# First layer in chunk groups of 2, 4, 4, 4, 2, with TensorE's order in the first group written out and the norm's scaling read from PSUM

## Chip, cores and metric

One core of a Trainium2 chip (trn2). The metric is the device time of one execution in microseconds, as the median of several runs; the time of the kernel before is 1269.53 us, the median of three runs from 1269.15 to 1269.59 us.

## The reference

```python
kv  = einsum('bhsd,bhse->bhde', k, v)            # B=4, H=8, S=576, D=64
out = einsum('bhsd,bhde->bhse', q, kv)
x   = out / sqrt(mean(out*out, -1) + 1e-6) * g   # -> [2304 tokens, 512]
h = x @ w_in                                     # 512 -> 2048, float64 weights
x = where(h > 0, h, exp(min(h, 0)) - 1) @ w_out  # 2048 -> 512
p = probs / (probs.sum(-1) + 1e-9)               # 4 experts
y = sum over e of p[:, e] * (relu(x @ w1[e]) @ w2[e])   # 512 -> 1024 -> 512
```

Three stages in a row: attention without softmax and with a norm per head, layer 1 with ELU, layer 2 with four weighted experts.

## The kernel before

The 2304 tokens are 18 tiles of 128, and these are 6 blocks (j) of T = 384 tokens. Every product is made of three matmuls on operands split into a high and a low part: hi·hi, hi·lo, lo·hi (`split`: the high part is a cast on ACT, the low part a subtraction on POOL or DVE). The program is written engine by engine through a framework that schedules the instructions itself: the order in which the functions are called is a priority, and a scheduler with a model of times decides what each engine issues next. After that every engine works through its own queue in order; loads and stores all go through SP's queue.

**Attention.** `emit_kv` multiplies the k and v tiles into ps_kv, the products of a batch are copied to kvd. `emit_o` multiplies a q tile with kvd into ps_o (L316), squares it (ACT, L324), copies it to x (ACT, L325), sums the squares (DVE, L326), forms mean + 1e-6 (L327, on POOL for ten tiles, on DVE for eight), takes the power −0.5 (POOL, L330) and scales x with it (L331, on POOL for nine tiles, on DVE for nine). `emit_x` transposes x on TensorE into ps_xT (L343) and splits the result, times g, into the high (ACT, L352) and low parts (DVE, L353) of xq, the operand of layer 1, 128x256 at a time.

**Layer 1.** d_ff is 16 chunks of 128. They are taken in 4 groups of 4; in a group each block j in turn gets its chunks: `emit_mm1` (12 matmuls into ps_h, L376 to L378), ELU (ACT, ACT, DVE L384), split into h, and two steps later `emit_mm2` (12 matmuls into the four banks ps_y, L395 to L397). After a block's last chunk of a group the four banks are copied to (first group, ACT L405) or added into (DVE, L407) the block's sum acc. A weight chunk arrives as 512 KB of float64 bits in one of two raw buffers, is turned into float32 by five DVE and two ACT steps (`float32_of`, L159 to L175) and split (`split_w`). Attention's steps hang on the steps of the first group by a table, `todo`: tile 17's xT comes with step 13 of 24.

**Layer 2** works on pairs of blocks. `make_forms` makes seven sums and differences ("forms") of a pair's quarter blocks of acc, splits them and stores them to DRAM; `stage_w1` (L203 to L206, DVE) and `split_w1` do the same for the weights. `emit_q` multiplies forms into ps_a, ps_b, ps_c (L422 to L424), `emit_m` makes the second product, weighted into acc (DVE, L488) with the probabilities that `emit_p` loads and normalizes. The forms of the first pair and the probabilities are called in layer 1's last group, 2 to 20 half steps into it.

Of the kernel before, what the change touches and what calls it, by code (L numbers as in the profile page):

```python
# [30 lines left out]
def attention_moe_kernel(  # L31
# [49 lines left out]
    form_p = ctx.enter_context(tc.tile_pool(name="form", bufs=8))  # L81
    raw_p = ctx.enter_context(tc.tile_pool(name="raw", bufs=2))
    w_p = ctx.enter_context(tc.tile_pool(name="w", bufs=NSLOT))
    tf_p = ctx.enter_context(tc.tile_pool(name="tf", bufs=1))
# [4 lines left out]
    x_p = layer1.enter_context(tc.tile_pool(name="x_late", bufs=4, side="right"))  # L89
    cv_p = layer1.enter_context(tc.tile_pool(name="cv", bufs=2, side="right"))  # L90
    h1_p = layer1.enter_context(tc.tile_pool(name="h1", bufs=3, side="right"))
# [15 lines left out]
    g_sb = const.tile([P, 1], F32, name="g_sb")  # L107
    ebias = const.tile([P, 2], F32, name="ebias")
# [4 lines left out]
    p_sb = const.tile([P, NTILE, E], F32, name="p_sb")  # L113
# [13 lines left out]
    groups = []  # L127
    w_in, w_out = w_in.bitcast(U32), w_out.bitcast(U32)
    for g in range(F1 // FG):
        groups.append((w_in, w_out, g * NF))  # L130
    N1 = len(groups)
    for g in range(E * F2 // FG):
        groups.append((w1, w2, g * NF))
    NG = len(groups)
# [3 lines left out]
    def load_w(g, ab, c):  # L138

        if (g, ab, c) in raws or g >= NG:  # L140
            return
        wide = 2 if g < N1 else 1
        r = raws[g, ab, c] = raw_p.tile([P, 512 * wide], U32 if g < N1 else F32, tag="raw", name="raw")
        n = groups[g][2] + c
        nc.sync.dma_start(out=r, in_=groups[g][ab][n * P:(n + 1) * P, :])

    def weights(g, ab, c):
        load_w(g, ab, c)
        r = raws[g, ab, c]
        return float32_of(r) if g < N1 else r  # L150

# [32 lines left out]
    def split_w(g, ab, c):  # L184

        r = weights(g, ab, c)
        w = wf[g, ab, c] = w_p.tile([P, 2, 512], F32R, tag="w", name="w")
        split(w[:, 0, :], w[:, 1, :], r, nc.gpsimd)
# [4 lines left out]
    staged = {}  # L193

    def stage_w1(g, f):

        if g >= NG:
            return
        r0, r1 = weights(g, 0, 2 * f), weights(g, 0, 2 * f + 1)
        tf = tf_p.tile([P, 4, HK], F32, tag="tf", name="tf")  # L200
        b11, b21, b12, b22 = r0[:, :HK], r0[:, HK:], r1[:, :HK], r1[:, HK:]
        sub = nc.vector.tensor_tensor
        sub(out=tf[:, 0, :], in0=b12, in1=b11, op=ALU.subtract)  # L203
        sub(out=tf[:, 2, :], in0=b22, in1=b12, op=ALU.subtract)
        sub(out=tf[:, 1, :], in0=b22, in1=tf[:, 0, :], op=ALU.subtract)
        sub(out=tf[:, 3, :], in0=b21, in1=tf[:, 1, :], op=ALU.subtract)  # L206
        staged[g, f] = r0, r1, tf

    def split_w1(g, f):
# [3 lines left out]
        w = wf[g, 0, f] = [w_p.tile([P, 2, 2, HK], F32R, tag="w", name="w1f") for _ in range(4)]  # L213
# [4 lines left out]
        split(w[3][:, 0, 0], w[3][:, 1, 0], r1[:, HK:], nc.gpsimd)  # L218

# [7 lines left out]
    def make_forms(p):  # L227
# [4 lines left out]
        def form(name, src, eng):  # L232
            if name not in fs:
                fs[name] = form_p.tile([P, 2, 2, T], F32R, tag="f", name="f")
# [5 lines left out]
        def sums(in0, in1, op, into=None):  # L240
            if into is None:
                if "h" in late:
# [18 lines left out]
    def load_forms(p):  # L261
        fs = forms[p] = {}
        for name in F_ORDER:
            f = fs[name] = form_p.tile([P, 2, 2, T], F32R, tag="f", name="f")
# [16 lines left out]
    def emit_kv(t, tags="cd"):  # L281
# [4 lines left out]
        for b, rows in parts(t):  # L286
            first, last = t == tiles_of[b][0], t == tiles_of[b][-1]
            if first:
                kv_bank[b] = bank(tags, "ps_kv")
# [13 lines left out]
        if t + 6 < NTILE:  # L303
            load("k", t + 6)
            load("v", t + 6)

    xn = {}

    def emit_o(t, tags="cd"):

        ps = bank(tags, "ps_o")
        load("q", t)
        qt = main["q", t].rearrange("p (n t) -> p n t", t=P)
        for hp in range(NHP):
# [5 lines left out]
        x = xn[t] = at_p.tile([P, H, D], F32, tag="x", name="x", bufs=5)  # L320
        sq = at_p.tile([P, H, D], F32, tag="sq", name="sq")
        s = at_p.tile([P, H], F32, tag="ss", name="ss", bufs=3)
        ps3 = ps.rearrange("p (h d) -> p h d", d=D)
        nc.scalar.activation(sq, ps3, AF.Square)  # L324
# [5 lines left out]
        nc.gpsimd.tensor_tensor(out=s, in0=s, in1=mhalf, op=ALU.pow)  # L330
# [3 lines left out]
        if t + 6 < NTILE:  # L334
            load("q", t + 6)

    def emit_x(t, tags="cd"):

        x = xn.pop(t)
# [21 lines left out]
    def new_acc(j, shape):  # L361
        acc[j] = (acc_p if j < 2 else late["acc"]).tile(shape, F32, tag=f"acc{j}", name="acc")
# [5 lines left out]
    def emit_mm1(g, j, c):  # L368
        ps = bank("ab", "ps_h")[:, :T]
        w = wf[g, 0, c]  # L370
        for kk in range(KD):
            cols = slice(kk * P, (kk + 1) * P)
            ah, al = w[:, 0, cols], w[:, 1, cols]
            x = xq[j][kk // 2]
            bh, bl = x[:, 0, kk % 2, :], x[:, 1, kk % 2, :]
# [3 lines left out]
        h = hs[g, j, c] = h1_p.tile([P, 2, T], F32R, tag="h", name="h")  # L379
# [6 lines left out]

    def emit_mm2(g, j, c):
        h, w = hs.pop((g, j, c)), wf[g, 1, c]
        hi, lo, bh, bl = h[:, 0, :], h[:, 1, :], w[:, 0, :], w[:, 1, :]
        first, last = c == 0, c == NF - 1  # L390
        if first:
            banks2[j] = [bank("efghcd" if "acc" in late else "efgh", "ps_y")[:, :T] for _ in range(KD)]
        for m, ps in enumerate(banks2[j]):
            cols = slice(m * P, (m + 1) * P)
            nc.tensor.matmul(ps, bh[:, cols], hi, start=first, stop=False)  # L395
            nc.tensor.matmul(ps, bh[:, cols], lo, start=False, stop=False)  # L396
            nc.tensor.matmul(ps, bl[:, cols], hi, start=False, stop=last)  # L397
# [67 lines left out]
    def emit_m(g, p, i):  # L465
# [3 lines left out]
        for c in range(NF):  # L469
            h, w = hs.pop((g, p, c, i)), wf[g, 1, c]  # L470
# [32 lines left out]

# [146 lines left out]
```

## Time and profile before

| | |
|---|---|
| median of three runs | 1269.53 us (1269.15 to 1269.59) |
| the profiled execution, its own time | 1270.84 us |
| its span in the profile | 1269.1 us, 16851 instructions |
| TensorE (PE) busy | 1219.2 us, 96% of the span |
| VectorE (DVE) busy | 616.5 us, 49% |
| ScalarE (ACT) busy | 454.9 us, 36% |
| GpSimd (POOL) busy | 383.7 us, 30% |
| chain that ended last | PE 88%, DVE 3%, POOL 2%, ACT 2%, DMA 2% |

The span is the time from the first to the last instruction that the profiler saw in one execution. A share is an average over stages with different limits: 96% of TensorE says nothing of where the other 4% lie, so the views by stretch of time are read first. A row of the view of groups gives the instruction's line, engine, operation, what it writes and reads, its shape and count, then its busy time in us and the mean of one in ns, and behind the second bar the idle time ahead of it with what ended it. The trace lacks a few per cent of the matmul records, so counts of matmuls are taken from the program.

### The profile page before, as it was taken

Reading aid. Unit: us, or ns where it says so; the run is one execution under the profiler, and the core shown is the slowest. Engines: PE = TensorE matmul, PEld = TensorE weight load, DVE = VectorE, ACT = ScalarE, POOL = GpSimd, SP = SyncE. Lnnn points to the kernel's source line nnn. Section 1 sums busy time; section 2 is a strip of 40 time slices with the busy share of each in tenths; the row PEclk is TensorE's granted clock in tenths of the full one; section 3 lists DMA queues with packets and bytes.
Section 4 is the critical chain, followed back from the end, with each engine's and each line's share of the span. In section 5 each row is a group of like instructions: output and inputs, shape, how many; then the busy total and the mean of one; then the engine's idle time right before and its main releaser. Section 6 shows DMA issues by size and latency. Waiting matters only on the chain.

```text
span 1269.1 us, 16851 instructions
## 1 busy us (share of the span) xinstructions
PE 1219.2 (96%) x6600; PEld 1130.8 (89%) x6600; DVE 616.5 (49%) x1019; ACT 454.9 (36%) x894; POOL 383.7 (30%) x330
## 2 busy tenths in 40 slices
PE   5789779999999999999999999999999999999998
PEld 4678779999999999899899898898898898888887
DVE  4776637427322262566445445445445445444443
ACT  3666546535434354334222222222222222222120
POOL 3465544325323374235203213212212222221000
PEclk9899889999999999999999999999999999999999
DMA  9623103102000041045541441441541441440551
GB/s 324 221 96 108 30 22 86 48 1 65 11 1 9 26 188 37 26 185 206 198 175 50 191 174 51 191 174 50 191 175 50 191 178 47 191 183 17 199 199 75
DMA packets 43887, 147.14 MB, mean 116 GB/s; under 512 B 7072, under 2 KB 7072, under 8 KB 43808
## 3 DMA queue, kind: packets, MB, share of 16 engines
q1 hardware_dynamic: 43808, 146.07, 31.9%
q8 instruction: 52, 0.85, 0.3%
q14 instruction: 27, 0.22, 0.1%
HBM read 124.82 MB, written 21.23 MB: 115 GB/s over the span
## 4 chain that ended last, share of the span: by engine, by line
PE 88%; DVE 3%; POOL 2%; ACT 2%; DMA 2%; issue 1%; SPq 0%; ACTq 0%; DVEq 0%; POOLq 0%
PE ps_y L475 11%; PE ps_y L476 11%; PE ps_y L477 10%; PE ps_y L396 5%; PE ps_y L397 5%; PE ps_y L395 5%; PE ps_h L376 5%; PE ps_h L377 4%; PE ps_h L378 4%; PE ps_a L422 3%; PE ps_a L424 3%; PE ps_a L423 3%; PE ps_c L423 3%; PE ps_c L424 3%; PE ps_c L422 3%; PE ps_b L424 3%
## 5 line engine op out<-in xcount | busy, mean ns | idle before, releaser
L476 PE MATMUL ps_y<-w,h 128*128 128x512 f32 x576 | 226.6, 393 | 0.0
L475 PE MATMUL ps_y<-w,h 128*128 128x512 f32 x576 | 225.4, 394 | 0.6 <-DVE acc L488 0.4
L477 PE MATMUL ps_y<-w,h 128*128 128x512 f32 x576 | 220.4, 395 | 0.0
L449 POOL TENSOR_TENSOR c<-u,p 128x384 f32<-128x384 f32 x48 | 48.8, 1017 | 411.9 <-DVE h L461 411.9
L461 DVE SCALAR_TENSOR_TENSOR h<-c,h 128x384 fp32r<-128x384 f32 x144 | 98.2, 682 | 138.1 <-ACT h L460 138.1
L180 POOL TENSOR_TENSOR h<-e,h 128x384 fp32r<-128x384 f32 x96 | 104.0, 1084 | 186.3 <-ACT h L179 169.0
L460 ACT ACTIVATE h<-c 128x384 fp32r<-128x384 f32 x144 | 75.5, 525 | 203.5 <-DVE c L446 72.6
L376 PE MATMUL ps_h<-x,w 128*128 128x384 f32 x384 | 131.9, 347 | 8.0 <-ACT w L179 4.3
L396 PE MATMUL ps_y<-h,w 128*128 128x384 f32 x384 | 131.0, 341 | 2.3 <-POOL h L180 2.3
L378 PE MATMUL ps_h<-x,w 128*128 128x384 f32 x384 | 131.6, 343 | 1.2 <-POOL w L180 1.2
L377 PE MATMUL ps_h<-x,w 128*128 128x384 f32 x384 | 132.0, 344 | 0.0
L397 PE MATMUL ps_y<-h,w 128*128 128x384 f32 x384 | 128.9, 341 | 0.0
L477 PEld LDWEIGHTS ps_y<-w,h 128*128 128x128 f32 x576 | 108.3, 188 | 22.6
L475 PEld LDWEIGHTS ps_y<-w,h 128*128 128x128 f32 x576 | 108.5, 188 | 20.5 <-DVE acc L488 0.8
L476 PEld LDWEIGHTS ps_y<-w,h 128*128 128x128 f32 x576 | 108.5, 188 | 20.2
L395 PE MATMUL ps_y<-h,w 128*128 128x384 f32 x384 | 124.1, 343 | 1.6 <-ACT acc L405 1.6
L488 DVE SCALAR_TENSOR_TENSOR acc<-ps_y,p_sb,acc 128x512 f32<-128x512 f32 x126 | 88.2, 745 | 72.7 <-PE ps_y L477 72.1
L384 DVE SCALAR_TENSOR_TENSOR e<-e,ps_h 128x384 f32<-128x384 f32 x96 | 52.7, 550 | 143.8 <-ACT e L383 137.2
L376 PEld LDWEIGHTS ps_h<-x,w 128*128 128x128 f32 x384 | 73.9, 193 | 10.3 <-ACT w L179 4.6
L382 ACT ACTIVATE e<-ps_h 128x384 f32<-128x384 f32 x96 | 47.0, 491 | 100.4 <-PE ps_h L378 95.7
L438 ACT COPY p<-ps_c 128x384 f32<-128x384 f32 x48 | 23.0, 480 | 148.2 <-PE ps_c L424 148.2
L378 PEld LDWEIGHTS ps_h<-x,w 128*128 128x128 f32 x384 | 74.1, 193 | 1.7 <-POOL w L180 1.7
(100 smaller groups left out, 2419.3 us busy)
## 6 DMA issues: line engine op xcount, KB each, us to landing
f<-kept SPq DMA_DIRECT2D x98, 768.0 KB, 7.9
raw<-in_moe_w_dram SPq DMA_DIRECT2D x64, 256.0 KB, 2.6
kept<-f SPq DMA_DIRECT2D x21, 768.0 KB, 3.6
raw<-in_moe_w_in_dram SPq DMA_DIRECT2D x16, 512.0 KB, 3.6
raw<-in_moe_w_out_dram SPq DMA_DIRECT2D x16, 512.0 KB, 3.7
qkv<-in_v_dram SPq DMA_DIRECT2D x18, 256.0 KB, 5.3
qkv<-in_k_dram SPq DMA_DIRECT2D x18, 256.0 KB, 5.4
qkv<-in_q_dram SPq DMA_DIRECT2D x18, 256.0 KB, 4.2
```

Of the source, the lines that this page charges most:

```text
L180: eng.tensor_tensor(out=lo, in0=src, in1=hi.bitcast(F32), op=ALU.subtract)
L376: nc.tensor.matmul(ps, ah, bh, start=(kk == 0), stop=False)
L377: nc.tensor.matmul(ps, ah, bl, start=False, stop=False)
L378: nc.tensor.matmul(ps, al, bh, start=False, stop=(kk == KD - 1))
L395: nc.tensor.matmul(ps, bh[:, cols], hi, start=first, stop=False)
L396: nc.tensor.matmul(ps, bh[:, cols], lo, start=False, stop=False)
L397: nc.tensor.matmul(ps, bl[:, cols], hi, start=False, stop=last)
L424: nc.tensor.matmul(ps, wl, xh, start=False, stop=stop and last, skip_group_check=True)
L461: nc.vector.scalar_tensor_tensor(out=lo, in0=ps, scalar=0.0, in1=hi.bitcast(F32), op0=ALU.max, op1=ALU.subtract,)
L475: nc.tensor.matmul(ps, hi[:, cols], bh, start=first, stop=False)
L476: nc.tensor.matmul(ps, hi[:, cols], bl, start=False, stop=False)
L477: nc.tensor.matmul(ps, lo[:, cols], bh, start=False, stop=last)
```

## The change

1. Layer 1's 16 chunks are taken in groups of 2, 4, 4, 4 and 2 in place of 4, 4, 4, 4. There are five groups, so five times instead of four a block's ps_y goes to acc: 24 more adds on DVE.
2. In the first group the matmuls of TensorE are tied together in the order in which they are called, by dependencies that cost no semaphore. The order per block j is: two o tiles of block j+1, `emit_mm1` of the first chunk, the third o tile, half of block j−1's ps_y (`emit_half`, two banks, both chunks), `emit_mm1` of the second chunk, some kv, the three xT of block j+1, the other half of ps_y. The other engines' orders are still the scheduler's.
3. The norm: `emit_o` squares ps_o, sums, adds 64·1e-6 (DVE for all tiles) and takes the power on POOL; `emit_x` scales straight from ps_o in PSUM on DVE (L325). The copy on ACT and the scalings on POOL are gone; the factor 8 that stands for the mean is in g8 = 8·g. The xT is split by one operation of 128x512 each on ACT and DVE (L338, L339).
4. Loads of k, v, q and of the first weights are called by a list. The first w_in chunk stands ahead of k and v tiles 2 to 4 on SP's queue.
5. The form buffers take the space of layer 1's x after layer 1; so `make_forms(0)` and `emit_p` are called behind the loop of layer 1. Layer 1's x, one tile per block, has six buffers, h four instead of three, acc four early ones instead of two.

```diff
-    POOL_MEAN = (1, 2, 3, 5, 8, 9, 12, 14, 16, 17)
-    POOL_SCALE = (2, 6, 8, 9, 10, 13, 15, 16, 17)
...
+    first_groups = [[0, 1]] + [list(range(n, n + NF)) for n in range(2, NC1 - 2, NF)] + [[NC1 - 2, NC1 - 1]]
...
     def emit_o(t, tags="dgh"):
...
         nc.scalar.activation(sq, ps.rearrange("p (h d) -> p h d", d=D), AF.Square)
-        nc.scalar.copy(x, ps3)
         nc.vector.tensor_reduce(out=s, in_=sq, op=ALU.add, axis=AX.X)
-        (nc.gpsimd if t in POOL_MEAN else nc.vector).tensor_scalar(
-            out=s, in0=s, scalar1=1.0 / D, scalar2=1e-6, op0=ALU.mult, op1=ALU.add
-        )
+        nc.vector.tensor_scalar_add(s, s, D * 1e-6)
         nc.gpsimd.tensor_tensor(out=s, in0=s, in1=mhalf, op=ALU.pow)
-        (nc.gpsimd if t in POOL_SCALE else nc.vector).tensor_tensor(
-            out=x, in0=x, in1=s.unsqueeze(2).to_broadcast([P, H, D]), op=ALU.mult
-        )
     def emit_x(t, tags="dgh"):
+        x = at_p.tile([P, H, D], F32, tag="x", name="x")
+        nc.vector.tensor_tensor(
+            out=x, in0=ps_o.pop(t).rearrange("p (h d) -> p h d", d=D),
+            in1=xn.pop(t).unsqueeze(2).to_broadcast([P, H, D]), op=ALU.mult,
+        )
...
-        for kh in range(2):
-            hi, lo = (xq[j][kh][:, a, :, i * P:(i + 1) * P] for a in (0, 1))
-            src = pt3[:, 2 * kh:2 * kh + 2, :]
-            nc.scalar.mul(hi, src, g_sb)
+        hi, lo = (xq[j][:, a, :, i * P:(i + 1) * P] for a in (0, 1))
+        nc.scalar.mul(hi, pt3, g8)
...
+    loads("k0-1 w1c0 k2-4 q0-2 w1c1")
...
+    for j in range(NB):
+        o = list(range(TT * (j + 1), TT * (j + 2))) if j + 1 < NB else []
+        for t in o[:2]:
+            emit_o(t)
+        emit_mm1(j, 0)
+        for t in o[2:]:
+            emit_o(t)
+        if j == 0:
+            split_w(0, 1, 0)
+        if j:
+            emit_half(j - 1, (0, 1))
+        emit_mm1(j, 1)
+        for t in more_kv.get(j, ()):
+            emit_kv(*t)
+        if j == 0:
+            split_w(0, 1, 1)
+        for t in o:
+            emit_x(t)
+        if j == NB - 2:
+            end_attention()
+        if j:
+            emit_half(j - 1, (2, 3))
...
+    emit_half(NB - 1, range(KD))
+    before = None
+    for i in traced[begin:]:
+        if isinstance(i, mybir.InstMatmult):
+            if before is not None:
+                tc.add_manual_dep(
...
     layer1.close()
+    late["form"] = ctx.enter_context(tc.tile_pool(name="form", bufs=8, side="right", reuse_waits="tile"))
...
+    make_forms(0)
+    emit_p()
```

What the two schedules make of it stands in the order of instructions of each engine; three places are shown. The first is TensorE's start, before: kv of the first batch, the first block's o, the first xT, and then the first layer-1 matmuls (ps_h).

```order
L294 MATMUL ps_kv<-qkv 64x64 x48
L316 MATMUL ps_o<-kvd,qkv 128x128 x12
L294 MATMUL ps_kv<-qkv 64x64 x24
L343 MATMUL ps_xT<-ident,x 128x128 x4
L294 MATMUL ps_kv<-qkv 64x64 x8
L343 MATMUL ps_xT<-ident,x 128x128 x8
L376 MATMUL ps_h<-x,w 128x384 x2
L316 MATMUL ps_o<-kvd,qkv 128x128 x4
```

The same of the change, up to its first ps_h:

```order
L292 MATMUL ps_kv<-qkv 64x64 x48
L310 MATMUL ps_o<-kvd,qkv 128x128 x12
L292 MATMUL ps_kv<-qkv 64x64 x16
L332 MATMUL ps_xT<-ident,x 128x128 x4
L292 MATMUL ps_kv<-qkv 64x64 x8
L332 MATMUL ps_xT<-ident,x 128x128 x4
L292 MATMUL ps_kv<-qkv 64x64 x8
L332 MATMUL ps_xT<-ident,x 128x128 x4
L310 MATMUL ps_o<-kvd,qkv 128x128 x4
L310 MATMUL ps_o<-kvd,qkv 64x128 x8
L361 MATMUL ps_h<-x,w 128x384
```

Two o tiles of the next block have moved ahead of the first ps_h. The second place is DVE's queue in the middle of attention, before (ss is the sum of squares, raw, m and x with raw the weight conversion, e the ELU):

```order
L326 TENSOR_REDUCE ss<-sq 128x8
L175 SCALAR_TENSOR_TENSOR m<-m,x 128x512
L327 TENSOR_SCALAR ss<-ss 128x8
L384 SCALAR_TENSOR_TENSOR e<-e,ps_h 128x384
L159 TENSOR_SCALAR x<-raw 128x512
L172 SCALAR_TENSOR_TENSOR x<-raw,x 128x512
L175 SCALAR_TENSOR_TENSOR m<-m,x 128x512
L384 SCALAR_TENSOR_TENSOR e<-e,ps_h 128x384
L331 TENSOR_TENSOR x<-x,ss 128x512
L159 TENSOR_SCALAR x<-raw 128x512
```

and of the change:

```order
L151 TENSOR_SCALAR x<-raw 128x512
L317 TENSOR_REDUCE ss<-sq 128x8
L319 TENSOR_SCALAR ss<-ss 128x8
L325 TENSOR_TENSOR x<-ps_o,ss 128x512
L369 SCALAR_TENSOR_TENSOR e<-e,ps_h 128x384
L317 TENSOR_REDUCE ss<-sq 128x8
L164 SCALAR_TENSOR_TENSOR x<-raw,x 128x512
L319 TENSOR_SCALAR ss<-ss 128x8
L167 SCALAR_TENSOR_TENSOR m<-m,x 128x512
L154 TENSOR_SCALAR m<-raw 128x512
L325 TENSOR_TENSOR x<-ps_o,ss 128x512
L151 TENSOR_SCALAR x<-raw 128x512
```

Sum, mean and scaling of every tile stand in this queue now, the scaling (L325) from ps_o, with conversion steps of a weight between them. The third place is DVE's queue at the end of layer 1, before (s are the sums of the forms, f their low parts); some twenty more rows of ELU and adds of layer 1 follow these:

```order
L246 TENSOR_TENSOR s<-acc 128x2x384
L246 TENSOR_TENSOR s<-s,acc 128x2x384
L384 SCALAR_TENSOR_TENSOR e<-e,ps_h 128x384
L180 TENSOR_TENSOR f<-s,f 128x768
L246 TENSOR_TENSOR s<-acc,s 128x2x384
L180 TENSOR_TENSOR f<-acc,f 128x768
L384 SCALAR_TENSOR_TENSOR e<-e,ps_h 128x384
```

and of the change, where the one L369 is the last ELU step of layer 1:

```order
L195 TENSOR_TENSOR tf<-raw 128x256
L196 TENSOR_TENSOR tf<-raw 128x256
L377 TENSOR_TENSOR acc<-ps_y,acc 128x384
L197 TENSOR_TENSOR tf<-raw,tf 128x256
L377 TENSOR_TENSOR acc<-ps_y,acc 128x384 x2
L198 TENSOR_TENSOR tf<-raw,tf 128x256
L377 TENSOR_TENSOR acc<-ps_y,acc 128x384
L172 TENSOR_TENSOR f<-s,f 128x768
L172 TENSOR_TENSOR f<-acc,f 128x768
L369 SCALAR_TENSOR_TENSOR e<-e,ps_h 128x384
L242 TENSOR_TENSOR s<-acc,s 128x2x384
```

The weights' staging (L195 to L198), four adds and two lows of forms stand directly ahead of the last ELU step now.

## Rows read from the trace of the kernel before

**Rows 1.** Windows: stretch, length, busy of PE, PEld, DVE, ACT, POOL, PEclk, DMA share, GB/s.

```profile
0.00:31.00 31.00, 16.47 (x197) 14.14 (x197) 12.62 (x24) 11.81 (x22) 11.57 (x17) 0.96 0.92 328
31.00:168.70 137.70, 108.32 (x728) 99.59 (x728) 99.42 (x168) 86.98 (x174) 75.72 (x61) 0.88 0.35 110
168.70:505.50 336.80, 336.28 (x1908) 335.91 (x1909) 139.81 (x229) 158.53 (x314) 131.97 (x113) 1.00 0.13 44
```

**Rows 2.** Groups by line, PE, 0 to 168.7 us: busy, mean ns | idle before.

```profile
L376 PE MATMUL ps_h<-x,w 128*128 128x384 f32 x76 | 28.3, 388 | 7.5 <-ACT w L179 4.3 <-DVE e L384 2.1 <-ACT x L352 1.1
L396 PE MATMUL ps_y<-h,w 128*128 128x384 f32 x48 | 16.9, 352 | 2.3 <-POOL h L180 2.3
```

**Rows 3.** Waits of PE over the span: total us, times, longest.

```profile
PE ps_xT L343 <- DVE x L331: 8.9, 5, 2.7
PE ps_xT L343 <- POOL x L331: 4.2, 2, 3.9
```

**Rows 4.** Timeline: start us, length us, instruction [idle <- releaser]. One tile, o to xT.

```profile
132.79 1.16 PE L316 MATMUL ps_o<-kvd,qkv 128*128 128x128 f32 x8 [0.40 <-ACT x L325]
140.60 1.81 POOL L330 TENSOR_TENSOR ss<-ss,mhalf 128x8 f32<-128x8 f32 x1
144.06 0.88 PE L343 MATMUL ps_xT<-ident,x 128*128 128x128 f32 x4 [2.72 <-DVE x L331]
```

**Rows 5.** Timeline of PE: o and xT of three other third tiles.

```profile
57.59 1.05 PE L316 MATMUL ps_o<-kvd,qkv 128*128 128x128 f32 x8
67.05 0.66 PE L343 MATMUL ps_xT<-ident,x 128*128 128x128 f32 x4 [1.16 <-DVE x L331]
73.37 1.95 PE L316 MATMUL ps_o<-kvd,qkv 128*128 128x128 f32 x16
88.50 0.66 PE L343 MATMUL ps_xT<-ident,x 128*128 128x128 f32 x4
154.51 1.16 PE L316 MATMUL ps_o<-kvd,qkv 128*128 128x128 f32 x8
165.97 1.11 PE L343 MATMUL ps_xT<-ident,x 128*128 128x128 f32 x4 [0.32 <-POOL x L331]
```

**Rows 6.** Timeline of PE: last xT of the start, first layer-1 matmuls.

```profile
29.25 1.11 PE L343 MATMUL ps_xT<-ident,x 128*128 128x128 f32 x4 [3.91 <-POOL x L331]
30.93 1.01 PE L376 MATMUL ps_h<-x,w 128*128 128x384 f32 x2 [0.56 <-ACT x L352]
```

**Rows 7.** Windows, columns as in rows 1, a stretch after a wait of PE.

```profile
48.73:55.55 6.82, 5.73 (x27) 4.97 (x28) 2.88 (x6) 4.56 (x8) 2.38 (x2) 0.50 0.44 135
```

**Rows 8.** Groups by line, DVE, over the span: busy us, mean ns | idle before.

```profile
L331 DVE TENSOR_TENSOR x<-x,ss 128x512 f32<-128x512 f32 x9 | 9.4, 1045 | 4.7 <-POOL ss L330 4.7
L488 DVE SCALAR_TENSOR_TENSOR acc<-ps_y,p_sb,acc 128x512 f32<-128x512 f32 x126 | 88.2, 745 | 72.7 <-PE ps_y L477 72.1
L407 DVE TENSOR_TENSOR acc<-ps_y,acc 128x384 f32<-128x384 f32 x72 | 37.2, 552 | 38.3 <-PE ps_y L397 38.3
L246 DVE TENSOR_TENSOR s<-s,acc 128x768 f32<-128x768 f32 x3 | 2.9, 952 | 0.0
L180 DVE TENSOR_TENSOR f<-acc,f 128x768 fp32r<-128x768 f32 x6 | 10.1, 1682 | 2.6 <-ACT f L179 2.6
L180 DVE TENSOR_TENSOR f<-s,f 128x768 fp32r<-128x768 f32 x3 | 3.9, 1293 | 0.3 <-ACT f L179 0.2
L203 DVE TENSOR_TENSOR tf<-raw 128x256 f32<-128x256 f32 x16 | 9.1, 568 | 15.9 <-DMA raw<-in_moe_w_dram 13.1 <-POOL w1f L180 2.6
L206 DVE TENSOR_TENSOR tf<-raw,tf 128x256 f32<-128x256 f32 x16 | 6.7, 422 | 0.4
L384 DVE SCALAR_TENSOR_TENSOR e<-e,ps_h 128x384 f32<-128x384 f32 x96 | 52.7, 550 | 143.8 <-ACT e L383 137.2 <-POOL f L180 4.2 <-POOL h L180 2.4
```

**Rows 9.** Waits of DVE, 0 to 171 us, for a raw weight.

```profile
DVE m L162 <- DMA raw<-in_moe_w_out_dram: 5.7, 3, 2.7
```

**Rows 10.** Waits of PE over the span, at the layer boundary.

```profile
PE ps_a L422 <- ACT p L432: 0.6, 1, 0.6
```

More of the change, by code (lines that the diff above doesn't have):

```diff
@@ L124, in load, with load_w, weights @@
         nc.sync.dma_start(out=r, in_={"q": q, "k": k, "v": v}[nm][t * P:(t + 1) * P, :])
-    groups = []
     w_in, w_out = w_in.bitcast(U32), w_out.bitcast(U32)
[L129 to L134, printed above, removed]
+    NC1 = F1 // P
+    first_groups = [[0, 1]] + [list(range(n, n + NF)) for n in range(2, NC1 - 2, NF)] + [[NC1 - 2, NC1 - 1]]
+    assert sum(map(len, first_groups)) == NC1
+    NG = E * F2 // FG
     raws = {}
-    def load_w(g, ab, c):
-        if (g, ab, c) in raws or g >= NG:
+    def load_w(layer, ab, n):
+        if (layer, ab, n) in raws:
             return
[L142 to L150, printed above, removed]
+        r = raws[layer, ab, n] = raw_p.tile([P, 512 * (2 - layer)], (U32, F32)[layer], tag="raw", name="raw")
+        src = ((w_in, w_out), (w1, w2))[layer][ab]
+        nc.sync.dma_start(out=r, in_=src[n * P:(n + 1) * P, :])
+    def weights(layer, ab, n):
+        load_w(layer, ab, n)
+        r = raws[layer, ab, n]
+        return r if layer else float32_of(r)
     def float32_of(r):
@@ L233, in form @@
             if name not in fs:
-                fs[name] = form_p.tile([P, 2, 2, T], F32R, tag="f", name="f")
+                fs[name] = late["form"].tile([P, 2, 2, T], F32R, tag="f", name="f")
             f = fs[name]
@@ L279, in attention_moe_kernel, with emit_kv @@
     kv_bank = {}
[L281 removed]
+    def emit_kv(t, only=None):
         load("k", t)
@@ L302, in emit_kv, with emit_o @@
                     )
[L303 to L311, printed above, removed]
+    ps_o, xn = {}, {}
+    def emit_o(t, tags="dgh"):
+        ps = ps_o[t] = bank(tags, "ps_o")
         load("q", t)
@@ new lines, in loads @@
+    def loads(text):
+        for n in text.split():
+            if n[0] == "w":
+                load_w(0, int(n[1]) - 1, int(n[3:]))
+            else:
+                for t in range(int(n[1:].split("-")[0]), int(n.split("-")[-1].lstrip("qkv")) + 1):
+                    for nm in {"q": "q", "k": "kv"}[n[0]]:
+                        load(nm, t)
+    traced = nc.cur_bb.bb.instructions
+    begin = len(traced)
+    loads("k0-1 w1c0 k2-4 q0-2 w1c1")
+    load_g()
+    for t in range(5):
+        emit_kv(t)
@@ new lines, in attention_moe_kernel @@
+    split_w(0, 0, 0)
+    for t in range(TT):
+        emit_o(t, "abd")
+    loads("k5-8 q3-5")
+    emit_kv(5)
+    emit_kv(6)
+    emit_x(0, "gh")
+    emit_kv(7)
+    emit_x(1, "gh")
+    split_w(0, 0, 1)
+    emit_kv(8)
+    emit_x(2, "gh")
+    loads("w2c0")
+    loads("k9-11")
+    loads("q6-8")
+    more_kv = {0: [(9,), (10,), (11,)], 1: [(12,), (13, 2)], 2: [(13, 3), (14,), (15,), (16,), (17,)]}
+    more_w = {0: [(1, 0)], 1: [(0, 2), (0, 3)], 2: [(1, 2)], 3: [(1, 3), (0, 4)], 4: [(0, 5), (1, 4)], 5: [(1, 5)]}
@@ new lines, in attention_moe_kernel @@
+    emit_half(NB - 1, range(KD))
[4 more added lines that the diff above has]
+                tc.add_manual_dep(
+                    i, before.name,
+                    mybir.DependencyInfo(mybir.DependencyClass.NoSync, mybir.DependencyReason.DATA),
+                    reason="order",
+                )
+            before = i
+    todo = {}
+    steps = []
+    for g, cs in list(enumerate(first_groups))[1:]:
+        begins = 2 * len(steps)
+        steps += [(g, j, c) for j in range(NB) for c in cs]
+        length = 2 * len(steps) - begins
+        if g + 1 < len(first_groups):
+            cs = first_groups[g + 1]
+            pieces = [p for i in range(0, len(cs), 2) for p in ((0, cs[i]), (0, cs[i + 1]), (1, cs[i]), (1, cs[i + 1]))]
+            for n, (ab, c) in enumerate(pieces):
+                todo.setdefault(begins + length * (n + 3) // (len(pieces) + 4), []).append((split_w, 0, ab, c))
```

182 lines of the change are left out of this document (87 added, 95 removed), and 17 rows, old and new, of tables (first, todo).

## The prediction

> **What bounds the kernel now.** I read the windows first. From 168.7 us on TensorE is busy all the time: 336.28 of 336.80 us in the rest of layer 1, at full clock [rows 1]. Before that it is not: from 31 to 168.7 us it is busy for 108.32 of 137.70 us, at a mean granted clock of 0.88 [rows 1]. The first 31 us are the DMA engines', busy for 0.92 of it [rows 1]. So the stretch between has most to give. It is the one in which attention (o, norm, xT) runs beside the first layer-1 products, and its matmul counts, 76 and 48 on one line of three each, say that (76+48)×3 = 372 of layer 1's 2304 matmuls are done when it ends [rows 2]. The dense stretch gives the price of a layer-1 matmul: 336.8/1908 = 0.1765 us.
>
> The waits of TensorE say what it lacks: mostly the normalized x, before a transposition to xT [rows 3]. A tile's chain shows why that comes late: o at 132.79, POOL's power at 140.60, xT at 144.06 after a wait for DVE's scaling, so 11.27 us from o to xT [rows 4]. Between them are a square on ACT, a sum on DVE, the power of 1.81 and a scaling; the power alone starts 7.8 us after o. What fills the rest is other work in the in-order queues of ACT, DVE and POOL, weight conversion and ELU, as the order of instructions shows.
>
> [...]
>
> DVE is busy for 139.81 of 336.80 us in the dense stretch [rows 1]: work added to it there costs nothing as long as TensorE is a few products ahead.
>
> **Part 1: attention ends earlier.** The change fixes TensorE's order in the first group: per block, two o tiles, 12 matmuls of ps_h, the third o, half the ps_y of the block behind, 12 more of ps_h, some kv, three xT, the other half. TensorE can't pass the xT, so the path is: third o, its chain to xT, then to the next third o. I walk it.
>
> The first ps_h matmul is at 30.93 us before, after a wait of 3.91 for POOL's scaling [rows 6]. That wait goes (POOL scales no more). A 512 KB weight load now stands ahead of k and v: at the 328 GB/s of the first 31 us [rows 1] that is 1.6. Two o tiles (1.05 us for one, [rows 5]), 2.1, stand before the ps_h now, of which about 1.2 lie in the 1.68 us from xT to ps_h [rows 6]: 0.9. So 30.93−3.91+1.6+0.9 = 29.5, and the third o of block 1 stands 12 matmuls later, at 31.6.
>
> Chain: the third tiles of four blocks took 9.46 us (57.59 to 67.05), 14.2 (from the second half of the group at 73.37, so 74.35, to 88.50), 11.46 (154.51 to 165.97) [rows 5] and 11.27 [rows 4]. I take their mean, 11.6: the copy on ACT (L325 of before) and the scaling on POOL go, but every scaling now stands in DVE's queue between the steps of the weight conversion, as the order shows. Five chains: 58.0. From the third xT to the next third o lie that xT (0.6), 12 ps_y (2.1), two o (2.1), 12 ps_h (2.1): 6.9, in the first of four stretches no ps_y: 25.5 in all. With 2.0 for the clock after four of the waits, 8.0, the last xT is at 31.6+58.0+25.5+8.0 = 123.1 us.
>
> By then the fixed order has issued 5 blocks of 24 ps_h matmuls and 84 of ps_y, 204 in all; before, 372 at 168.7. The 168 that are missing cost 168×0.1765 = 29.7 us. So **part 1 is 123.1+29.7−168.7 = −15.9 us.** Bounds: chains of 9.46 take 10.7 us more off, chains of 14.2 put 13.0 on.
>
> **Scaling from PSUM.** Of the operation itself only DVE's forms bear on it: 1045 ns mean over nine from SBUF (L331), 745 over 126 from PSUM of the same size (L488) [rows 8]. So 0.3 us less each, which lies within the spread of the chain and enters no term. [...] The one 128x512 hi and lo in place of two of 128x256 each save an instruction's start on ACT and DVE; that too is inside the chain's spread.
>
> **Part 2: groups.** Five groups of chunks instead of four add 24 accumulating adds on DVE (L407): 24×0.552 = 13.2 us [rows 8], hidden under the dense stretch, where DVE idles for 197 us. If that cover failed they would cost up to their 13.2. The first group is only two chunks long, so the second group's weights are wanted sooner: I put **+1.5** on new small waits there, between 0 and 5 (two waits the length of the worst conversion wait, 2.7 [rows 9]).
>
> **Part 3: the boundary of the layers.** Before, the forms of the first pair were made inside layer 1's last group, beside dense matmuls; the boundary has a wait of 0.6 [rows 10]. Now they come after the last group's loop, because their space is that of layer 1's x. DVE's order at the boundary has, ahead of the last ELU step: one sum (0.95), two lows (1.68 and 1.29), four staging steps (2×0.568+2×0.422 = 1.98), four adds (2.21), and the ELU step itself (0.55) [rows 8]: 8.7 us. TensorE has 30 matmuls in hand, 5.3 us. First wait: 3.4, for the PSUM bank that the ELU step frees. Then four forms follow one by one, each a wait between 0.6 [rows 10] and one low on DVE, 1.68 [rows 8]; I take 1.0, so 4.0. Less the 0.6 of before: **+6.8**. From below 2 (the sum falls out, the four waits hide), from above 12.8: 3.4, four lows (6.7), and three more sums (3.3), less 0.6. The probabilities' load stands behind seven stores of forms on SP now, and its sums in DVE's queue; they are wanted only with layer 2's first accumulation, after all form products of its first half group, so I put nothing on them; if they came late, the price is one more wait of the kind that the upper bound holds. Layer 2 is otherwise as it was.
>
> **Sum:** −15.9+1.5+6.8 = −7.6 us. The profiled execution's own time is 1270.84, its span 1269.1, the median of the three runs 1269.53; the span lies 0.4 under the median and I move the median by the sum: **1261.9 us.** What a measurement of this kernel can tell from no change is about 0.2%, 2.5 us.
>
> **Rivals.**
> *Chains shrink more.* With POOL rid of ten scalings and means and ACT of 18 copies (10.6 us), each third tile may take 9.46 us: −7.6−10.7 = −18.3, **1251.2 us**. For it: both groups of waits are for the scaling, one of them for POOL's [rows 3]. Against: ELU and conversion stay in the same queues.
> *The boundary eats the gain.* At its upper bound of 12.8: −15.9+1.5+12.8 = −1.6, **1267.9 us**. For it: seven lows and four sums stand on two engines with nothing else for TensorE to do. Against: the products take the forms one after another, and TensorE works between them.
> [...]
> *Slower: DVE's queue blocked by a weight that is not there.* DVE works in order, and in the fixed part of the program conversion steps of a weight (L151 to L167) stand between reduction and scaling. Where the raw weight is late, what stands behind, the scaling and so xT, is late too, and TensorE can't go round it any more; the scheduler's freedom hid that before. Such a wait was up to 2.7 us [rows 9]. Raw weights have two buffers, so a load waits for the conversion before it, and the q, k and v loads queue behind it on SP. One in each of four blocks is 10.8 us: −7.6+10.8 = +3.2, **1272.7 us**. It decides from 10.1 us of such waits in all (7.6+2.5). For it: DVE, ACT and POOL stay the busiest engines there; against: loads are issued blocks ahead, and DMA is busy for a third [rows 1].
> That the change does not do what it says is no rival: the order of instructions shows it.
>
> **How the numbers follow.** Forecast 0.58, chains shrink 0.14, boundary 0.11, clock 0.06, blocked queue 0.11. The forecast's own spread leaves 0.02 within 0.2% and 0.01 slower. Faster by over 0.2%: 0.55+0.14 = 0.69; within: 0.02+0.11+0.06 = 0.19; slower: 0.01+0.11 = 0.12. The range goes from the short chains, 1251.0, to a little beyond the blocked queue, 1274.0; about half of the first case, and what would be worse than the last, is left out.
>
> **What would show it.** Right: the last xT (L332) near 123 us; 204 layer-1 matmuls by then; dense PE from there to layer 2's first form product near 495 us (the 2100 matmuls left take 370.7, less the few that stand behind it); there a wait of some 3 us for the bank freed by DVE's e and about four of 1 us; no waits of DVE for the new adds. Wrong: waits of xT for DVE that end on a conversion step's DMA (blocked queue), a clock under 0.85 from 31 to 123 us (clock), a boundary of over 10 us, or a last xT later than 135.

## The result and the profile after

The change takes 1251.03 us (median of four runs, 1248.69 to 1252.67) against 1269.56 of the kernel before: a ratio of 0.9853, with a 95% interval of 0.9836 to 0.987. That is −18.5 us where −7.6 was forecast, just inside the low end of the range, and at the time of the first rival, 1251.2. The profiled execution took 1251.78 us with a span of 1249.7, so I compare spans: −19.4.

The windows of the changed kernel (columns as in rows 1), cut at the last xT and at the layer boundary:

```profile
30.00:111.80 81.80, 66.32 (x547) 62.78 (x544) 74.52 (x133) 59.07 (x112) 53.91 (x37) 0.92 0.45 152
111.80:482.00 370.20, 366.71 (x2096) 364.79 (x2095) 159.29 (x278) 172.35 (x337) 132.60 (x118) 0.99 0.11 33
482.00:500.00 18.00, 14.95 (x62) 13.82 (x63) 11.89 (x18) 6.82 (x13) 11.61 (x9) 0.81 0.95 333
```

Attention ends 12 us earlier than forecast, at 111.8 and not 123. By then TensorE has done what the program's order says, 40 and 28 matmuls on one line of three each, so (40+28)×3 = 204 of layer 1 (groups of PE, 0 to 111.8 us):

```profile
L361 PE MATMUL ps_h<-x,w 128*128 128x384 f32 x40 | 14.0, 350 | 0.0
...
L383 PE MATMUL ps_y<-h,w 128*128 128x384 f32 x28 | 10.8, 387 | 0.0
```

So part 1 is 111.8+29.7−168.7 = −27.2 us, by the prediction's own sum. The rest of the span's −19.4 is then +7.8, where 1.5+6.8 = 8.3 was forecast. TensorE's waits over the span show the boundary too, the bank that the ELU step frees first:

```profile
PE ps_xT L332 <- DVE x L325: 18.0, 11, 2.8
...
PE ps_b L422 <- DVE e L369: 2.9, 1, 2.9
PE ps_d L423 <- DVE f L172: 2.3, 2, 1.5
PE ps_y L383 <- DVE acc L377: 2.0, 2, 1.2
```

The first of these lines answers to [rows 3]: eleven waits for the scaling, and none for POOL's. What VectorE did in front of one of them is in its timeline around block 4, whose third o stands at 80.43 and its xT at 91.03:

```profile
84.31 0.67 DVE L317 TENSOR_REDUCE ss<-sq 128x8 f32<-128x512 f32 x1
84.91 1.11 DVE L161 SCALAR_TENSOR_TENSOR m<-raw,m 128x512 f32<-128x512 uint32 x1
85.94 1.48 DVE L151 TENSOR_SCALAR x<-raw 128x512 uint32<-128x512 uint32 x1
87.34 0.68 DVE L325 TENSOR_TENSOR x<-ps_o,ss 128x512 f32<-128x512 f32 x1
87.94 0.16 DVE L319 TENSOR_SCALAR ss<-ss 128x8 f32<-128x8 f32 x1
...
90.19 0.69 DVE L325 TENSOR_TENSOR x<-ps_o,ss 128x512 f32<-128x512 f32 x1
```

The third tile's sum ends at 84.98, and its 0.16 us addition starts at 87.94: two steps of a weight conversion (L161, L151) and another tile's scaling stand between. From 30 to 111.8 VectorE is busy for 74.52 of 81.80 us. Most of what it converts there is not wanted there yet. The first group needs 4 weight chunks and the second 8; in the order of VectorE's instructions the changed kernel has 16 conversions begun before the last xT, the kernel before 19 or 20. A conversion is five steps, by their means in this stretch 3.46 us of VectorE: 0.732 (L151), 0.436 (L154), 0.772 (L161), 0.770 (L164) and 0.752 (L167).

### The profile page after: what moved, and what is told of

It reads as the page before. It is cut to its first block, busy times and chain, and to the rows that moved or that the text cites. A ratio compares the mean times of both kernels' runs of the same rounds, so it can differ in the third digit from the quotient of the medians.

```text
span 1249.7 us, 16813 instructions
## 1 busy us (share of the span) xinstructions
PE 1209.2 (97%) x6600; PEld 1122.0 (90%) x6600; DVE 618.7 (50%) x1044; ACT 444.2 (36%) x858; POOL 368.1 (29%) x312
## 4 chain that ended last, share of the span: by engine, by line
PE 89%; DVE 6%; DMA 1%; ACT 1%; issue 1%; POOL 1%; SPq 0%; POOLq 0%; DVEq 0%; ACTq 0%
PE ps_y L475 11%; PE ps_y L476 11%; PE ps_y L477 10%; PE ps_h L361 5%; PE ps_y L384 5%; PE ps_y L385 5%; PE ps_y L383 5%; PE ps_h L362 5%; PE ps_h L363 5%; PE ps_a L422 3%; PE ps_b L422 3%; PE ps_a L424 3%; PE ps_a L423 3%; PE ps_b L424 3%; PE ps_c L424 3%; PE ps_b L423 3%
## 5 line engine op out<-in xcount | busy, mean ns | idle before, releaser
L461 DVE SCALAR_TENSOR_TENSOR h<-c,h 128x384 fp32r<-128x384 f32 x144 | 95.7, 665 | 140.8 <-ACT h L460 140.8
L172 POOL TENSOR_TENSOR h<-e,h 128x384 fp32r<-128x384 f32 x96 | 101.7, 1060 | 202.4 <-ACT h L171 189.4
L384 PE MATMUL ps_y<-h,w 128*128 128x384 f32 x384 | 131.4, 342 | 0.0
L385 PE MATMUL ps_y<-h,w 128*128 128x384 f32 x384 | 131.3, 342 | 0.0
L383 PE MATMUL ps_y<-h,w 128*128 128x384 f32 x384 | 129.2, 344 | 2.0 <-DVE acc L377 2.0
L361 PE MATMUL ps_h<-x,w 128*128 128x384 f32 x384 | 130.3, 339 | 0.2
L362 PE MATMUL ps_h<-x,w 128*128 128x384 f32 x384 | 129.4, 337 | 0.0
L363 PE MATMUL ps_h<-x,w 128*128 128x384 f32 x384 | 129.2, 337 | 0.0
L369 DVE SCALAR_TENSOR_TENSOR e<-e,ps_h 128x384 f32<-128x384 f32 x96 | 52.8, 550 | 136.4 <-ACT e L368 136.3
L383 PEld LDWEIGHTS ps_y<-h,w 128*128 128x128 f32 x384 | 73.4, 192 | 2.6 <-DVE acc L377 2.6
L377 DVE TENSOR_TENSOR acc<-ps_y,acc 128x384 f32<-128x384 f32 x96 | 50.1, 553 | 49.7 <-PE ps_y L385 49.5
L384 PEld LDWEIGHTS ps_y<-h,w 128*128 128x128 f32 x384 | 74.1, 193 | 0.0
```

Source lines behind the costliest of these rows:

```text
L172: eng.tensor_tensor(out=lo, in0=src, in1=hi.bitcast(F32), op=ALU.subtract)
L361: nc.tensor.matmul(ps, ah, bh, start=(kk == 0), stop=False)
L362: nc.tensor.matmul(ps, ah, bl, start=False, stop=False)
L363: nc.tensor.matmul(ps, al, bh, start=False, stop=(kk == KD - 1))
L461: nc.vector.scalar_tensor_tensor(out=lo, in0=ps, scalar=0.0, in1=hi.bitcast(F32), op0=ALU.max, op1=ALU.subtract,)
```

## The experiments

Theory A is that the end of attention goes by the work in VectorE's queue. The rivals are that the chain's own delays set it (B), that the fixed order of TensorE made the gain (C), and that the scaling from PSUM did (D). In what follows "conversions" are those before the last xT in VectorE's order. Each time is a median of four runs; those of the changed kernel lie between 1248.69 and 1252.67, so a difference of 2 us or less is not read as one.

**The fixed order away.**

```diff
-    before = None
-    for i in traced[begin:]:
...
-            before = i
```

> The changed kernel without the ties between TensorE's matmuls in the first group; all else as it is. In the changed kernel VectorE is busy for 73.9 of the 81.1 us from the first layer-1 matmul to the last xT, at 111.1 us. Theory A (VectorE's amount of work sets when attention ends): its order holds the same 15 weight conversions before the last xT, so the last xT stays within 6 us of 111 and the time within 0 to +5 us of 1251. Rival C (the fixed order of TensorE does it): last xT at 125 us or later, time +8 us or more.

1247.06 us (ratio 0.9826, 0.9812 to 0.9841), 4.0 less than the change, where A had 0 to 5 more; last xT at 109.7, 15 conversions. C falls: the fixed order does not gain, it costs here. TensorE waits for the scaling for 4.5 us in place of 18.0, and the granted clock is higher (columns as above):

```profile
30.00:109.70 79.70, 69.70 (x540) 62.26 (x537) 73.30 (x128) 58.61 (x113) 54.18 (x37) 0.98 0.46 156
```

It is 0.98 there, not 0.92.

**Conversions held back**, to 8 and to 4 in the changed kernel, and to 8 in the kernel before. The first steps of a later conversion are ordered behind the last xT's low part on VectorE, and the calls are put off (the lines are those of 8 in the changed kernel):

```diff
+        if NTILE - 1 in xlo:
+            tc.add_manual_dep(
+                nc.cur_bb.bb.instructions[-1], xlo[NTILE - 1].name,
...
-    more_w = {0: [(1, 0)], 1: [(0, 2), (0, 3)], 2: [(1, 2)], 3: [(1, 3), (0, 4)], 4: [(0, 5), (1, 4)], 5: [(1, 5)]}
+    more_w = {1: [(0, 2)], 2: [(0, 3)], 3: [(1, 2), (0, 4)], 4: [(1, 3), (0, 5)], 5: [(1, 4), (1, 5)]}
```

> The changed kernel with 8 instead of 15 or 16 weight conversions before the last xT; the others are ordered behind it in VectorE's queue. Theory A: 7 or 8 conversions of 3.46 us are 24 to 28 us of VectorE's work less; the last xT comes at about 100 us (the fastest chains, 8.2 us times 5, and the stretches between them as measured, 28 us, on 32.8), the time falls by 7 to 11 us to 1240 to 1244. Rival B (the chain's own delays set it, not the amount of VectorE's work): last xT at 109 to 113 us, time 1249 to 1253.

> As the run with 8 conversions, with only 4 before the last xT. Theory A: the last xT at 96 to 101 us, hardly earlier than with 8 since VectorE is no bound any more; then 8 conversions of 3.46 us, 28 us, are wanted within 15 us of layer-1 work that is left, so TensorE waits for weights: time 1240 to 1250. Rival B: last xT at 109 to 113 us, time 1249 to 1260.

> The kernel before, with 8 instead of 19 weight conversions ahead of its last xT (at 166 us), and nothing else of the change. Theory A: 11 conversions of 3.46 us, 38 us of VectorE's work, leave the stretch; the last xT comes 20 to 35 us earlier and the time falls by 8 to 20 us. Rival C (the fixed order of TensorE and attention one block ahead are needed): the last xT within 8 us of 166, time within 4 us of 1269.5.

With 8: 1233.32 us (0.9718, 0.9704 to 0.9733), 17.7 less than the change, last xT at 97.3. That is more than expected, and the best kernel of this study. With 4: last xT at 98.1, but 1242.96 us. The kernel before with 8: 1252.37 us (0.9869, 0.9854 to 0.9883), 17 us less without anything else of the change, last xT at 141.5 in place of 166.7. The windows of the two changed kernels, 8 first, then 4:

```profile
30.00:97.30 67.30, 62.56 (x535) 59.70 (x536) 50.12 (x93) 46.29 (x91) 42.19 (x30) 0.97 0.39 136
...
120.00:130.00 10.00, 10.00 (x59) 10.00 (x59) 6.55 (x13) 6.92 (x14) 4.79 (x4) 1.00 0.36 109
```

```profile
30.00:98.10 68.10, 63.61 (x551) 60.60 (x552) 41.05 (x75) 40.51 (x80) 36.78 (x26) 0.97 0.30 105
...
120.00:130.00 10.00, 6.94 (x36) 6.13 (x36) 6.78 (x12) 5.22 (x9) 3.99 (x4) 1.00 0.35 105
```

VectorE's 24 us less work (74.52 to 50.12) bring the last xT forward by 14.5; another 9 us less bring nothing, and TensorE then waits for weights (6.94 of 10 us busy in one stretch of the second group). B falls. But a conversion is also two steps on ACT and a cast of its high part there, and ACT's work falls with it, from 59.07 to 46.29 us. The runs that hold conversions back relieve both queues, and none of them says how much of the 14.5 us is VectorE's.

**Both**: 8 conversions and a free order.

> The run with 8 weight conversions before the last xT, and TensorE's order in the first group left to the scheduler as well. The free order was worth 4 us with 15 conversions, the 8 conversions 18 us in the fixed order. If the two act on the same waits (VectorE's work sets the end of attention, and a free TensorE only fills its holes), they add up in part: 1229 to 1233 us, last xT at 94 to 99 us. If the fixed order is what let TensorE profit from the 8 conversions: 1236 us or more.

1237.94 us, last xT at 101.6: 4.6 more than with the fixed order. So the fixed order costs 4.0 us with 16 conversions ahead of the last xT, and gains 4.6 with 8.

**More work on VectorE, and on POOL,** off the chain:

```diff
+        nc.vector.tensor_reduce(out=more, in_=x, op=ALU.add, axis=AX.X)
```

```diff
+        nc.gpsimd.tensor_tensor(out=more, in0=x[:, 0:4, :], in1=x[:, 0:4, :], op=ALU.subtract)
```

> The changed kernel with one reduction of 128x512 more per tile on VectorE, behind the low part of xT, with a result that nothing reads. It is off the chain of its tile. Theory A (VectorE's amount of work sets the end of attention): 15 times 0.68 us is 10.2 us more between 30.6 us and the last xT, which comes at 118 to 122 us, time 1258 to 1262. Rival B (the chain's own delays): last xT at 110 to 113 us, time 1250 to 1253.

> The changed kernel with one subtraction of 128x256 more per tile on POOL, behind the low part of xT, with a result that nothing reads: some 0.75 us each, 11 us on POOL in place of VectorE. Theory A: last xT at 109 to 114 us, time 1249 to 1254. Rival (POOL's power and low parts are the link that is late): last xT at 117 us or later, time 1256 or more.

VectorE: last xT at 116.2, 1253.54 us; of 10.2 us of work, 4.4 reach the last xT and 2.5 the time. That lies between A and B. POOL: 112.3 and 1251.93, so more work on POOL does not matter. The same on the kernel with 8 conversions, where VectorE is busy for 74%:

> The run with 8 conversions before the last xT (1233.3 us, last xT 97.3), with one more reduction of 128x512 per tile on VectorE off the chain. In the changed kernel, with VectorE busy for 91% of the stretch, these cost 4.4 us at the last xT and 2.5 us of the time. Here VectorE is busy for 50.1 of 67.3 us, 74%. Theory A (VectorE is full): its holes take the reductions up, last xT at 97 to 99 us, time 1233 to 1235. Theory A2 (VectorE need not be full; what stands in its queue ahead of a scaling delays it one for one): last xT at 101 to 103 us, time 1236 to 1238.

1237.87 us, last xT at 101.4: 4.1 later, although VectorE has holes. So A holds in the second form that the text above calls A2: VectorE need not be full; what stands in its queue ahead of a sum, an addition or a scaling delays that tile, though not one for one: 4.1 of some 10 us. This is shown for work added on VectorE; ACT's queue is tried by the copy in the next group.

**The scaling as before**: copied on ACT, from SBUF, nine tiles on POOL.

```diff
+        nc.scalar.copy(xs[t], ps.rearrange("p (h d) -> p h d", d=D))
...
+        (nc.gpsimd if t in (2, 6, 8, 9, 10, 13, 15, 16, 17) else nc.vector).tensor_tensor(
+            out=x, in0=x, in1=xn.pop(t).unsqueeze(2).to_broadcast([P, H, D]), op=ALU.mult
```

The second run is with all 18 on VectorE, the third with ACT's copy alone, whose result nothing reads, and the scaling from PSUM.

> The changed kernel with the scaling as before: a copy of ps_o on ACT, the scaling from SBUF, on POOL for nine tiles and on VectorE for nine. VectorE has 9 operations of 0.685 us less, 6 us in all, and those left were 1.045 us from SBUF. Theory A: the last xT at 105 to 113 us, time 1247 to 1253. Rival D (the scaling straight from PSUM made the chains short): last xT at 117 us or later, time 1256 or more.

> As the run with the scaling from SBUF, but all 18 scalings on VectorE. If POOL's nine scalings, in POOL's queue, are what costs: 1250 to 1254, last xT at 111 to 115 us. If it is the copy, or that VectorE reads SBUF while POOL does (1.045 us instead of 0.685, 18 times 0.36 is 6.5 us): 1256 us or more, last xT at 117 us or later.

> The changed kernel with the copy of ps_o on ACT kept (18 times 0.59 us, 10.6 us), its result not read; the scaling stays straight from PSUM. With the copy, and the scaling from SBUF on POOL and VectorE, the time was 8.7 us longer and the last xT at 123.2 us. If ACT's copy is what costs: 1256 to 1260, last xT at 118 to 123 us. If not: 1250 to 1254, last xT at 111 to 114 us.

1259.72 us (0.9924, 0.9909 to 0.9939), last xT at 123.2; 1260.78, 122.5; 1255.28, 116.9, between what was expected with and without a price of the copy. So the scaling from PSUM is worth 8.7 us here. About half of that is work on ACT (4.3): 18 copies of 0.59, off the tile's own chain, bring the last xT 5.1 later (with one conversion more ahead of it), about as much as 10.2 us on VectorE did. So by this run it is not VectorE's queue alone that attention goes by. The other half is left for the read of SBUF and for the wait for the copy, and no run takes these two apart; POOL's nine scalings cost nothing that shows. The scaling itself, on VectorE, of the all-VectorE kernel and of the change, from the view of one line (least, median and largest ns):

```profile
L327 DVE TENSOR_TENSOR x<-x,ss x18: 678/690/1741, 20.0 to 120.9; 128x512 f32<-128x512 f32 x18
```

```profile
L325 DVE TENSOR_TENSOR x<-ps_o,ss x18: 675/683/692, 21.6 to 110.3; 128x512 f32<-128x512 f32 x18
```

From SBUF the same operation takes up to 1741 ns, from PSUM never over 692. These runs have 17 conversions (16 in the change), so the comparison was made again with 8 in each:

> The changed kernel, TensorE's order fixed, with 8 conversions before the last xT and the scaling from SBUF as before. The three other kernels with 8 conversions are at 1233.3 (fixed, PSUM), 1237.9 (free, PSUM) and 1235.8 us (free, SBUF). If the scaling from PSUM shortens the chain in a fixed order by itself, by what the run with SBUF showed: 1240 to 1243, last xT at 105 us or later. If most of that was the queue's other work, one conversion more among it: 1232 to 1237, last xT at 97 to 101 us.

1245.29 us, last xT at 108.7, 12.0 more than from PSUM. So the scaling's worth in the fixed order is not the one conversion.

**Neither the fixed order nor the scaling from PSUM**, then also the old widths and loads (the parts of xT 128x256, the first weight behind k and v 0 to 4), then the first with 8 conversions.

> The changed kernel with both the scaling as before (copy on ACT, from SBUF, nine on POOL) and TensorE's order left to the scheduler. What is left of the change are the groups of 2, 4, 4, 4, 2, the loads, the widths of xT's parts and the forms behind layer 1. If the two parts add up (8.7 and -4.0 us): 1254 to 1257 us, so the rest of the change is worth 13 us. If the scaling from PSUM matters only because the fixed order makes TensorE wait for it: 1247 to 1251. If the rest is worth nothing: 1266 to 1270.

> As the run without the fixed order and with the scaling from SBUF (1244.0 us), and in addition the parts of xT in two operations of 128x256 each again, and the first weight's load behind k and v tiles 0 to 4 again. What is left are the groups with attention one block ahead, and the forms behind layer 1. Before the last xT the schedule has 18 weight conversions now, not 14. If groups and the order of the calls carry the gain: 1243 to 1247. If each conversion ahead of the last xT costs 1.5 to 2.4 us as in the two runs that held them back: 1250 to 1254. If loads and widths carry it: 1262 or more.

> As the run without the fixed order and with the scaling from SBUF (1244.0 us, 14 conversions before the last xT), with 8 conversions there. If VectorE's conversions still stand in the way of attention there: 6 times 1.5 to 2.4 us, so 1230 to 1235. If a free TensorE has filled those holes already: 1241 to 1247.

1243.98 us (1241.17 to 1246.99), last xT at 112.1 with 14 conversions, so 7.1 less than the change and below all that was expected; 1256.93, 122.4 with 18; 1235.83, 102.8 with 8. The parts do not add up: with a free order the scaling from PSUM gains nothing (1247.06 with it, 1243.98 without; at 8 conversions 1237.94 and 1235.83). Without both parts the kernel is still 25.5 us under the one before, so what is left, the groups with attention one block ahead, the loads, the widths and the fewer conversions ahead of the last xT, is enough for the change's gain. The run with old widths and loads has 4 conversions more, so what widths and loads do by themselves stays open.

**The boundary**: ACT's and VectorE's steps of the first forms behind the last ELU.

```diff
+    for i in traced[begin:]:
+        for b in last_of.values():
+            if i.engine == b.engine:
+                tc.add_manual_dep(
+                    i, b.name,
...
```

> The changed kernel with all ACT and VectorE steps of the first pair's forms ordered behind the last ELU of layer 1. At the boundary TensorE waits 2.9 us for the bank that this ELU frees, then 2.3 us for lows of forms and 0.8 for VectorE's sums in layer 2. If the boundary's cost is the place of the ELU in the queue: the 2.9 us go, time 1247 to 1249. If it is the amount of work that ACT and VectorE have there: the wait for the ELU goes and the lows come as much later, time 1250 to 1253.

1253.03 us (1249.57 to 1253.57). The wait for the ELU is gone in the profiled execution, the one of 1249.57, and others stand in its place:

```profile
PE ps_c L426 <- POOL f L172: 1.1, 1, 1.1
...
PE ps_a L426 <- DVE f L172: 1.0, 1, 1.0
PE ps_y L478 <- ACT h L463: 1.0, 2, 0.6
PE ps_b L425 <- DVE u L446: 0.8, 1, 0.8
```

The windows from 470 to 515 us, of the change and then of this run:

```profile
470.00:515.00 45.00, 38.63 (x185) 35.08 (x185) 28.28 (x44) 16.29 (x30) 20.23 (x14) 0.92 0.45 159
```

```profile
470.00:515.00 45.00, 40.07 (x189) 33.79 (x187) 34.54 (x49) 17.52 (x32) 23.68 (x15) 0.96 0.48 164
```

TensorE is idle there for 4.9 us in place of 6.4. So most of the boundary's waiting moves to other places with the step. That speaks for the amount of work there; what the place of the step is worth lies inside the spread of the runs and stays open.

## Why the prediction was right in direction and wrong in size

**Where TensorE loses time and that attention would end earlier**: right. 204 matmuls were done at the last xT, as forecast. The price of the 168 missing ones was a little high: 1908 counts the records of the trace, and the program has 2304−372 = 1932 matmuls in that stretch, so 0.1743 us each and 29.3 us in place of 29.7.

**The chain, the step that failed.** I carried 11.6 us per chain over from before, and wrote that the scaling from PSUM "enters no term". Third o to third xT took 8.65, 8.23, 11.52, 10.60 and 11.45 us: 50.5 for five against 58.0. For one, o and xT of block 1's third tile in TensorE's timeline:

```profile
32.76 1.05 PE L310 MATMUL ps_o<-kvd,qkv 128*128 128x128 f32 x8
...
41.41 1.08 PE L332 MATMUL ps_xT<-ident,x 128*128 128x128 f32 x4 [2.23 <-DVE x L325]
```

With the scaling as before they took 10.12, 10.73, 11.44, 10.79 and 11.59, 54.7 in all, and the first third o and the last xT stand here:

```profile
36.31 1.05 PE L310 MATMUL ps_o<-kvd,qkv 128*128 128x128 f32 x8
...
122.45 1.12 PE L333 MATMUL ps_xT<-ident,x 128*128 128x128 f32 x4 [4.58 <-POOL x L327]
```

So 4.2 us of the chains' 7.5 are the part that I had put at nothing. The other 3.3 are there without it: the mean of four rows, of which one was 14.2, was too long. The part's whole worth is 8.7 us of the 10.9 that the forecast missed, since the start and the stretches between chains get shorter with it as well. I had priced the instruction (0.3 us) and not the copy's work in ACT's queue nor what its SBUF operand costs. That the last xT of that run, at 122.45, meets my sum of 123.1 is luck: its start is 4.7 later than my 31.6, its chains are 3.3 and its stretches, 31.5, are 2.0 shorter.

Beneath that lies what I took as given, the "other work" in the queues: it was for the most part conversions that nothing waited for yet, and each one held back gave 1.5 us (before, 16.6 us for 11) to 2.2 us (the change, 17.7 for 8). With 8 of them the five chains took 8.62, 8.29, 9.30, 6.52 and 6.52 us, 39.3 in all.

**Stretches and clock, the other term that was too large.** From third xT to the next third o it took 5.9, 6.6, 6.8 and 8.7 us, 28.0 against 33.5 with the 8.0 that I had put on the clock there: 2.5 over the bare 25.5. No run shows a loss of 2.0 us to the clock after each of four waits; in its place the runs showed these 2.5, some 0.6 for each stretch, and a granted clock of 0.92. The clock's whole loss from 30 to 111.8 us, an estimate by that 0.92, is 0.08×81.8 = 6.5 us, and some of it lies inside the chains, whose times I had read from rows that held it already, so I had counted that twice. Against both stands the start: the third o of block 1 came at 32.76, 1.2 later than forecast. Together 7.5+5.5−1.2 = 11.8 us of the 12.

**Dense phase and boundary**: +7.8 against +8.3, the first wait 2.9 against 3.4. The sum is right, its parts less so. The +1.5 for small waits in the second group did not come: no wait of TensorE stands between 111.8 and 470 us. From 470 to 515 us it is idle for 6.4 us. 2.0 of them are the two waits for adds of ps_y in the list above: not all adds of the fifth group hide, as I had written. In place of four waits of 1.0 behind the first stands one of 1.5. And the granted clock of 0.81 from 482 to 500 us, which no term held, costs some 3 us (an estimate: 0.19 of 14.95 busy).

**The rivals.** "Chains shrink more" gave the time, in part by luck: its chains of 9.46 were 10.1, which is 7.5 us and not 10.7, and the smaller loss to the clock made up for it. Of its reasons the copy on ACT was borne out; that POOL is rid of its scalings gained nothing that shows. The boundary did not eat the gain. The blocked queue did not come as described: VectorE has no wait for a weight's DMA in the stretch. But the same conversions cost the change time by being there too early, not too late. The clock: 0.92 in the fixed order (30 to 111.8 us), so not under the 0.85 that was to show its rival, and 0.98 in the free one (30 to 109.7 us); a loss of 6.5 us in the fixed one, less than the 8.0 that I had put on it.

**PSUM against SBUF.** An operand in PSUM did not make the scaling longer here: 683 ns median from PSUM (the change), 690 from SBUF (all 18 on VectorE), and 675 and 678 at the least.

## What to carry to other kernels

Ask not only what an instruction costs but what stands in front of it in its engine's queue, and whether that is wanted yet: a scheduler that fills an engine with work for later can hold up the chain that TensorE waits for, and holding that work back took 17 us off either kernel. How much of that was VectorE's queue and how much ACT's is not shown; work added to either one delayed the chain (10.2 us on VectorE brought the last xT 4.4 us later, 18 copies of 0.59 on ACT 5.1). Count it in the order of instructions; too little ahead is a price too (4 conversions were worse than 8 by 9.6 us). Parts of a change need not add up: fixing one engine's order cost 4.0 us with crowded queues and gained 4.6 with cleared ones, and the scaling from PSUM paid only in the fixed order. And a sum that meets a measured time can do so by errors that cancel: compare term by term.

## What the runs showed of the hardware

An operation of VectorE with both operands in SBUF varied from 678 to 1741 ns for the same 128x512, with one from PSUM from 675 to 692. What POOL was doing when it began tells the two apart. In the kernel with all 18 scalings on VectorE from SBUF, six took 0.83 to 1.74 us, and each of the six began while a subtraction of POOL (L172) was running; none of the other twelve did, and they took 0.68 to 0.69. One of the six:

```profile
58.19 1.26 POOL L172 TENSOR_TENSOR w<-m,w 128x512 fp32r<-128x512 f32 x1
58.26 1.74 DVE L327 TENSOR_TENSOR x<-x,ss 128x512 f32<-128x512 f32 x1 [1.53 <-POOL ss L322]
```

In the changed kernel nine of the 18 scalings from PSUM began in that way, and they took 0.68 to 0.69 us as the others did:

```profile
100.73 1.29 POOL L172 TENSOR_TENSOR w<-m,w 128x512 fp32r<-128x512 f32 x1
100.79 0.69 DVE L325 TENSOR_TENSOR x<-ps_o,ss 128x512 f32<-128x512 f32 x1 [0.73 <-POOL ss L320]
```

The six lost 4.9 us together (against 0.68 each); that has the size of the 5.5 us between the run with all scalings on VectorE and the one with ACT's copy alone, but no run shows that it is the same.

The conversion's L151 has one operand, in SBUF, and its twelve executions between 30 and 112 us took from 410 to 1482 ns with a median of 428. The four over 1.1 us began while a subtraction of POOL was running, the other eight did not. The 1.48 us of the timeline further up began at 85.94, half a microsecond into this one:

```profile
85.43 1.71 POOL L172 TENSOR_TENSOR w<-m,w 128x512 fp32r<-128x512 f32 x1
```

The prediction took means of such rows for the price of an operation; with POOL at work beside it, the mean holds two prices. The 1045 ns of [rows 8] is the mean of nine scalings on VectorE, five of 0.68 to 0.69 us and four of 1.02 to 1.76; these four began while a subtraction of POOL was running, the five did not.
